# A fused channel-attention and GELU feed-forward kernel: three engines held to one written order, and the fourth feed-forward group of every chunk through the plain second layer

## Chip, core and metric

The kernel runs on one core of a Trainium2 chip. The metric is the device time of one execution in microseconds (us). The kernel before takes 2385.68 us in the median of three runs (2384.44 to 2390.18).

## What is computed

The shapes are four batches of 6080 tokens with 256 channels, all in 32-bit floats, and a feed-forward width of 2048.

```python
qn = q / (norm(q, axis=1) + 1e-6)           # norms over the 6080 tokens
kn = k / (norm(k, axis=1) + 1e-6)
s = kn.transpose(0, 2, 1) @ qn / tau        # 256 x 256 for each batch
a = softmax(s, axis=-1)
x = (v @ a).reshape(4 * 6080, 256)
h = x @ w_in                                # 256 -> 2048
g = 0.5 * h * (1 + erf(h / sqrt(2)))        # GELU
out = g @ w_out                             # 2048 -> 256
```

## The kernel before

**Products in parts.** Each 32-bit operand of a product is split into a high part that TensorE takes as it is and a low part for the rest (`his` and `los` for the activations, `whs` and `wls` for the first layer's weights). A product is then three matmuls: high weights by low activations, high by high, low by high. ScalarE (ACT) makes a high part by a copy or by the GELU itself, and VectorE (DVE) makes the low part by a subtraction, so every low part waits for a copy of ACT.

**Attention.** v @ a @ w_in is done as v @ (a @ w_in), so each batch has its own first-layer weights. While the chunks of batch b run, the kernel also prepares batch b+1: `load_qk`, `split_qk` and `burst` build the 256 x 256 scores, `norm_part` sums the squares for the norms, `softmax` runs in stages, and `w_group` makes the new weights. All this is hung between the steps of batch b by `extras`, by step numbers.

**Steps.** The tokens of a batch are cut in 12 chunks of four times 256 columns (the last two of four times 240), and the 2048 hidden features in 4 groups of 512. A step is one chunk and one group. There are 184 of them, since the first two chunks of the first batch go another way, at the start. In each step the first layer (`chunk_products`) is a Strassen-Winograd scheme: 7 products in place of 8, each 6 matmuls of 256 columns, 42 in all. They accumulate in few PSUM banks: `one` (a buffer of `ph`), `two` (the other buffer of `ph`), `px` and `pz`. Between the products ACT copies `one` to `px` (L585) and `two` to `p` (L590), and DVE adds `one` and `p` into `pz` (L594) and into `p` (L600). The third product (T2) goes on accumulating in `one`, so it may not start before the copy to `px` has read it; the fifth likewise waits for the sum into `pz`, the last for the sum into `p`.

**GELU and the second layer's forms.** Four blocks come out: B22 from `px`, B11 from `p`, B21 from `pz`, B12 from `one`. `block` applies the GELU twice to each, once to full precision into `gs` and once into the high part `his` (L565, L569), and DVE makes `los` (L570). The second layer is again a Strassen-Winograd scheme of 7 products (`chunk_out`), 42 matmuls of 256 columns. It needs four sums of the blocks, T1 to T4, which `sums` makes: three subtractions on DVE (L574, L576, L577), two casts on ACT (L575, L578), two subtractions on DVE (L579, L580). The second layer of a step runs between the first-layer products of the next step (`second`). It gathers four groups in the PSUM banks `po`, and after the fourth the result is joined (L725 to L737) and sent out.

**The plain way.** `plain_out(b, c)` is true for the last chunk of batches 0 to 2. There the second layer is 8 plain products of 3 matmuls with 480 columns, 24 in all, and T1 to T4 are not made. Instead B12 needs its high and low part too.

**What sets the order.** The kernel's calls go to a scheduler, which places each engine's instructions by priority and by a model of the durations, within the data's dependencies. Each engine runs its own list in that order and waits at the first instruction whose operands aren't ready.

**Loads.** Every step reads the second layer's weights again from DRAM (`load_part`, four buffers `wo`, four loads a step, two in a plain one). `norm_part` loads a slice of k or q into the one buffer `kqc` and sums it on ACT (L222) in the same step. All transfers are issued from SyncE (SP).

Of the kernel before, what the change touches and what calls it, by code (L numbers as in the profile page):

```python
# [9 lines left out]
F32 = mybir.dt.float32  # L10
# [38 lines left out]
CROSS = (("S4", "B22"), ("A11", "B11"), ("A12", "B21"), ("S3", "T3"), ("S1", "T1"), ("S2", "T2"), ("A22", "T4"))  # L49
SLOT = {"T2": 0, "T4": 1, "T1": 2, "T3": 3, "B12": 3, "B11": 4, "B22": 5, "B21": 6}  # L50
GSLOT = {"B11": 0, "B12": 1, "B22": 2, "B21": 3}
BLOCK = {(1, 0): "B22", (0, 1): "B11", (1, 1): "B21", (0, 0): "B12"}

# [16 lines left out]
def channel_attention_gelu_ffn(ctx, tc, qk, kqt, vt, tau, w_in, w_out, out):  # L70
# [20 lines left out]
    ps_h = ctx.enter_context(tc.tile_pool(name="ps_h", bufs=2, space=bass.MemoryType.PSUM))  # L91
    ps_x = ctx.enter_context(tc.tile_pool(name="ps_x", bufs=1, space=bass.MemoryType.PSUM))
    ps_o = ctx.enter_context(tc.tile_pool(name="ps_o", bufs=4, space=bass.MemoryType.PSUM))
# [27 lines left out]
    def bank():  # L121
        state["bank"] = at = (state.get("bank", -1) + 1) % 4
        if at % 2 and "halves" not in state:
            return ps_x.tile([P, NT], F32, name="px" if at == 1 else "pz")
        return ps_h.tile([P, NT], F32, name="ph")
# [42 lines left out]
    def qk_fill():  # L168
        state["fill"] = s = ps_o.tile([P, NCT, C], F32, name="po")
# [21 lines left out]
    def split_qk(b, js):  # L191
        raw = raws.pop((b, js))
        hl = pqk.tile([P, 2, JS, 2, C], F32R, name="hl")
        nc.scalar.copy(out=hl[:, 0], in_=raw)
        nc.vector.tensor_tensor(out=hl[:, 1], in0=raw, in1=f32(hl[:, 0]), op=ALU.subtract)
        hls[b, js] = hl


    def burst(b, k, m):
        cs = slice(m * P, (m + 1) * P)  # L200
        s = bank()
        ops = [(hls[b, k * NB + t], j) for t in range(NB) for j in range(JS)]
        for i, (hl, j) in enumerate(ops):
# [3 lines left out]
                             stop=(i == len(ops) - 1), skip_group_check=True)  # L207
        if k == 0:
# [7 lines left out]
    def norm_part(b, t, c):  # L216
# [4 lines left out]
        nc.sync.dma_start(out=x, in_=kqt[b, t, :, c * NS:(c + 1) * NS])  # L221
        nc.scalar.activation(out=x, in_=x, func=AF.Square, accum_out=state["nsum"][:, t, c:c + 1])  # L222

# [10 lines left out]
    def narrow(hi, lo, raw):  # L234
# [7 lines left out]
        else:  # L242
            state["nt"] = not state.get("nt")
            tmp = pg.tile([P, 2, n], F32, name="kqc" if state["nt"] else "pq", bufs=1)
# [37 lines left out]
    def plain_out(b, c):  # L282
        return c == NCH - 1 and b < B - 1

    def parts(b, c):
        return ((1, 3), (6, 8)) if plain_out(b, c) else ((0, 2), (2, 4), (4, 6), (7, 8))

    def load_part(b, c, g, i):
        at, to = parts(b, c)[i]
# [35 lines left out]
    def softmax(first, pool, name):  # L325
# [14 lines left out]
        if first:  # L340
            nps, acc = ps_o.tile([P, NT], F32, name="po"), state.pop("acc")
# [11 lines left out]
        if first:  # L353
            preload(AF.Exp, y)
        nc.vector.reciprocal(out=z, in_=y)
# [9 lines left out]
        rq = pool.tile([P, NT], F32, name=name)  # L365
        nc.tensor.matmul(rq[:, 0:C], ones, diag.rearrange("p h d -> p (h d)"), start=True, stop=True)
        for m in range(NCT):
# [6 lines left out]
        for m in range(NCT):  # L374
            e = pm.tile([P, C], F32, name=f"e{m}")
            den = dens[:, m:m + 1]
            nc.scalar.activation(out=e, in_=ts[m], func=AF.Exp, bias=nms[:, m:m + 1], accum_out=den)
            nc.vector.tensor_scalar(out=den, in0=den, scalar1=1e-9, scalar2=None, op0=ALU.add)
            nc.vector.reciprocal(out=rden[:, m:m + 1], in_=den)
            es.append(e)  # L380
        yield
        tp = pool.tile([P, NT], F32, name=name)
        tpv = tp.rearrange("p (d c) -> p d c", d=NCT)
        for m in range(NCT):
            for d in range(NCT):
                nc.tensor.transpose(out=tpv[:, d, m * P:(m + 1) * P], in_=es[m][:, d * P:(d + 1) * P],
                                    identity=ident)
        eh = pm.tile([P, NCT, C], F32R, name="eh")
        el = pm.tile([P, NCT, C], F32R, name="el")
        marks["eh"] = nc.scalar.copy(out=eh, in_=tpv)  # L390
        if first:
            preload(AF.Gelu, eh[:, 0, 0:2])
        marks["el"] = nc.vector.tensor_tensor(out=el, in0=tpv, in1=f32(eh), op=ALU.subtract)
# [17 lines left out]

    def w_group(b, g):

        eh, el = state["e"]
        win = wins.pop((b, g))
# [3 lines left out]
        for m in range(NCT):  # L419
            cs = slice(m * P, (m + 1) * P)  # L420
            pwt = bank()
            for d in range(NCT):
# [15 lines left out]
    def w_sums(g, tmp, first):  # L438
# [8 lines left out]
        for to, of in ((slice(0, 3), slice(1, 4)), (slice(3, 7), slice(4, 8))):  # L447
            if first and to.start == 0:
                continue
# [515 lines left out]
```

## Time and profile before

| | |
|---|---|
| median of 3 runs | 2385.68 us |
| time of the profiled execution | 2383.55 us |
| its span, first to last instruction | 2381.6 us |
| TensorE: matmuls | 16624 |
| VectorE busy, instructions | 1984.6 us, 2879 |
| ScalarE busy, instructions | 1640.7 us, 2788 |
| bytes moved | 504.51 MB |

PE is TensorE's matmuls and PEld its weight loads, which overlap them. The span lies inside the execution; 1.95 us of the profiled time are outside it. A matmul's row shows a duration longer than the distance to the next matmul, since matmuls overlap in the pipeline. So the work of PE is read from the distance of the starts. A row's text in brackets gives the idle time ahead of it and what ended it.

### The profile page before, as it was taken

What the parts mean: (1) busy time and instruction counts of PE and PEld (TensorE: products, weight loads), DVE (VectorE), ACT (ScalarE), POOL (GpSimd) and SP (SyncE); (2) the same over time, 40 slices, a digit from 0 to 9 for tenths busy, and PEclk for the clock granted to TensorE, in tenths of its full rate; (3) what the DMA queues carried; (4) which work ended last, traced back from release to release, by engine and by line L of the source; (5) the groups of instructions that cost most, each with busy time, mean ns of one, the idle gap of its engine ahead of it and who ended that gap; (6) DMA issues with size and microseconds to landing.
All of it is one profiled execution on the core that took longest, in us unless ns stands there. A gap on an engine that the chain in (4) does not pass through costs nothing.

```text
span 2381.6 us, 42310 instructions
## 1 busy us (share of the span) xinstructions
PE 2225.0 (93%) x16624; PEld 2110.3 (89%) x16624; DVE 1984.6 (83%) x2879; ACT 1640.7 (69%) x2788; POOL 48.5 (2%) x32
## 2 busy tenths in 40 slices
PE   8888999998899999999889999999988999999987
PEld 7768989998889889899879989898988999999987
DVE  6978888898679888889768988788876889899876
ACT  5647777776577677776657777677665667677764
POOL 0250000000000000000000000000000000000000
PEclk9999999999999999999999999999999999999998
DMA  9456777765456676775546677676554565666553
GB/s 379 160 194 234 258 243 261 240 208 177 166 194 226 238 235 233 250 255 191 168 159 206 228 235 245 228 256 230 169 174 144 166 211 191 214 206 207 192 171 133
DMA packets 162406, 504.51 MB, mean 212 GB/s; under 512 B 16672, under 2 KB 26912, under 8 KB 160160
## 3 DMA queue, kind: packets, MB, share of 16 engines
q1 hardware_dynamic: 162208, 501.81, 62.4%
q8 instruction: 131, 2.15, 0.4%
q14 instruction: 67, 0.55, 0.1%
HBM read 464.26 MB, written 37.49 MB: 211 GB/s over the span
## 4 chain that ended last, share of the span: by engine, by line
PE 50%; ACT 15%; DMA 15%; DVE 14%; issue 4%; POOL 1%; SPq 1%; POOLq 0%; ACTq 0%; DVEq 0%
DMA kqc<-kqt 12%; PE po L716 8%; PE po L713 7%; PE po L715 7%; PE ph L555 6%; PE ph L559 5%; PE ph L557 5%; ACT gs L565 4%; ACT his L569 4%; ACT kqc L222 2%; ACT his L578 2%; DVE gs L574 2%; DMA v_raw<-vt 2%; DVE los L580 2%; PE px L555 1%
## 5 line engine op out<-in xcount | busy, mean ns | idle before, releaser
L713 PE MATMUL po<-his,wo 128*128 128x256 f32 (+1 forms) x2408 | 691.6, 289 | 21.2 <-ACT his L578 13.3
L716 PE MATMUL po<-los,wo 128*128 128x256 f32 (+1 forms) x2408 | 677.9, 290 | 21.6 <-DVE los L580 12.2
L715 PE MATMUL po<-his,wo 128*128 128x256 f32 (+1 forms) x2408 | 681.0, 284 | 0.0
L555 PE MATMUL ph<-vhi,wl 128*128 128x256 f32 (+1 forms) x1840 | 533.4, 291 | 79.2 <-ACT px L585 41.9
L570 DVE TENSOR_TENSOR los<-gs,his 128x512 fp32r<-128x512 f32 (+1 forms) x564 | 381.1, 684 | 215.4 <-ACT his L569 211.8
L557 PE MATMUL ph<-vhi,wh 128*128 128x256 f32 (+1 forms) x1840 | 515.1, 280 | 0.0
L559 PE MATMUL ph<-vlo,wh 128*128 128x256 f32 (+1 forms) x1840 | 513.9, 280 | 0.0
L713 PEld LDWEIGHTS po<-his,wo 128*128 128x128 f32 x2408 | 463.1, 192 | 35.0 <-ACT his L578 21.0
L716 PEld LDWEIGHTS po<-los,wo 128*128 128x128 f32 x2408 | 453.4, 192 | 37.4 <-DVE los L580 17.2
L715 PEld LDWEIGHTS po<-his,wo 128*128 128x128 f32 x2408 | 462.4, 192 | 0.2
L555 PEld LDWEIGHTS ph<-vhi,wl 128*128 128x128 f32 x1840 | 350.5, 191 | 104.6 <-ACT px L585 47.2
L557 PEld LDWEIGHTS ph<-vhi,wh 128*128 128x128 f32 x1840 | 351.8, 191 | 1.9
L559 PEld LDWEIGHTS ph<-vlo,wh 128*128 128x128 f32 x1840 | 349.3, 190 | 0.0
L580 DVE TENSOR_TENSOR los<-gs,his 128x1024 fp32r<-128x1024 f32 (+1 forms) x172 | 208.9, 1215 | 54.9 <-ACT his L578 54.4
L578 ACT CAST his<-gs 128x1024 fp32r<-128x1024 f32 (+1 forms) x172 | 178.8, 1040 | 90.0 <-DVE gs L577 88.6
L565 ACT ACTIVATE gs<-px 128x512 f32<-128x512 f32 (+1 forms) x184 | 108.9, 592 | 181.2 <-DVE los L580 83.6
L575 ACT CAST his<-gs 128x1024 fp32r<-128x1024 f32 (+1 forms) x172 | 180.3, 1048 | 52.3 <-DVE gs L574 52.2
L579 DVE TENSOR_TENSOR los<-gs,his 128x1024 fp32r<-128x1024 f32 (+1 forms) x172 | 208.6, 1213 | 7.3 <-ACT his L575 7.0
L574 DVE TENSOR_TENSOR gs<-gs 128x1024 f32<-128x1024 f32 (+1 forms) x172 | 208.4, 1211 | 4.4 <-ACT gs L565 4.2
L590 ACT COPY p<-ph 128x512 f32<-128x512 f32 (+1 forms) x184 | 107.4, 583 | 65.0 <-PE ph L559 64.2
L565 ACT ACTIVATE gs<-p 128x512 f32<-128x512 f32 (+1 forms) x184 | 115.6, 628 | 40.7 <-DVE p L600 40.6
L594 DVE TENSOR_TENSOR pz<-ph,p 128x512 f32<-128x512 f32 (+1 forms) x184 | 126.9, 690 | 18.2 <-PE ph L559 15.2
(248 smaller groups left out, 4195.7 us busy)
## 6 DMA issues: line engine op xcount, KB each, us to landing
wo<-keep_out SPq DMA_DIRECT2D x540, 512.0 KB, 4.2
raw<-qk SPq DMA_DIRECT2D x95, 512.0 KB, 5.7
wo<-keep_out SPq DMA_DIRECT2D x172, 256.0 KB, 4.1
kqc<-kqt SPq DMA_DIRECT2D x72, 512.0 KB, 5.4
v_raw<-vt SPq DMA_DIRECT2D x20, 1024.0 KB, 5.2
out<-osb SPq DMA_DIRECT2D x40, 512.0 KB, 3.0
win<-keep_in SPq DMA_DIRECT2D x12, 1024.0 KB, 4.9
keep_in<-win SPq DMA_DIRECT2D x4, 1024.0 KB, 4.8
```

The lines of the kernel that those rows point to most:

```text
L555: nc.tensor.matmul(o, wls[g][:, a, q], vh[:, at, :h], start=start and q == 0, stop=False, skip_group_check=True)
L557: nc.tensor.matmul(o, whs[g][:, a, q], vh[:, at, :h], start=False, stop=False, skip_group_check=True)
L559: marks["product"] = nc.tensor.matmul(o, whs[g][:, a, q], vl[:, at, :h], start=False, stop=stop, skip_group_check=True)
L565: nc.scalar.activation(out=whole, in_=src, func=AF.Gelu)
L570: tt(out=lo, in0=whole, in1=f32(hi), op=ALU.subtract)
L574: tt(out=t[:, 0:2], in0=t[:, 1:3], in1=t[:, 0:2], op=ALU.subtract)
L578: nc.scalar.copy(out=hi[:, 0:2], in_=t[:, 2:4])
L579: tt(out=lo[:, 2:4], in0=t[:, 0:2], in1=f32(hi[:, 2:4]), op=ALU.subtract)
L580: tt(out=lo[:, 0:2], in0=t[:, 2:4], in1=f32(hi[:, 0:2]), op=ALU.subtract)
L713: nc.tensor.matmul(o, w[:, 1, q], mh, start=first and i % 2 == 0 and q == 0, stop=False, skip_group_check=True)
L715: nc.tensor.matmul(o, w[:, 0, q], mh, start=False, stop=False, skip_group_check=True)
L716: nc.tensor.matmul(o, w[:, 0, q], ml, start=False, stop=last and q == 1, skip_group_check=True)
```

## The change

**One written order.** The chunk loop no longer runs code in the order of its calls. `chunk_ops`, `chunk_out` and `join_ops` return small functions, each for one operation or one product. For every step they get a planned time, PE's products one after another at `D` = 0.71 apart, the operations of ACT and DVE at offsets from the ends of the products. The work for the next batch and the next chunk (`later`) gets places in the same plan. The list is sorted by planned time and emitted in that order, and each instruction of PE, ACT and DVE (`PINNED`) is bound to follow the one before it on its engine. SP's and POOL's instructions stay with the scheduler. The start of the program, up to the first step, is not bound.

**Group 4 is plain.** `plain_out(g)` is now true for group index 3 of each chunk of each batch, and no longer depends on the chunk. 46 steps are plain, against 12 before; 3 are plain in both. For 43 steps T1 to T4 go away, and 9 steps that were plain (groups 0 to 2 of the last chunk in batches 0 to 2) get them. The products of a chunk are gathered in other halves of the banks (`PLACE`), so that the plain products add into banks `po0` and `po1`, and the join needs two copies and five sums.

**Buffers and places.** The PSUM banks get fixed names: `pa` and `pb` take the place of the two buffers of `ph` and change roles at every step. `p5` has one buffer in place of two, and `pq` is gone into a larger `osb`. The load of `kqc` is planned one step ahead of its sum (`norm_load`, `norm_sum`), and `raw` is split one block in each step rather than two in one. The loads of `wo` are taken from one list (`todo`), always four ahead.

```diff
+PINNED = (mybir.EngineType.PE, mybir.EngineType.Activation, mybir.EngineType.DVE)
...
-    def plain_out(b, c):
-        return c == NCH - 1 and b < B - 1
+    def plain_out(g):
+        return g == NWG - 1
...
-    def chunk_products(b, c, g):
+    def chunk_ops(c, g, n):
...
+            if i == 0:
+                new("one", ps_h, "pb" if n % 2 else "pa")
+            if i == 1:
+                state["spare"] = "pa" if n % 2 else "pb"
+                new("two", ps_h, state["spare"])
...
+        copy, join = join_ops(b, c)
+        put(n + 1, "act0", copy, 2)
+        put(n + 1, "act0", copy, 3)
+        put(n + 1, "dve0", join, 0)
+        put(n + 1, "dve0", join, 1)
+        put(n + 1, "o5", join, 2)
+        put(n + 1, "dve3", join, 3)
+        put(n + 2, "dve1", join, 4)
...
+        for i in range(2 * NCT * NSC):
+            put(n0 + 8 + i, "load", norm_load, b, *divmod(i, NSC))
+            put(n0 + 9 + i, "act2", norm_sum, b, *divmod(i, NSC))
...
+    D = 0.71
...
+        if len(outs) == 8:
+            row = [0, "o", "o", 1, "o", 2, "x", "o", 3, "o", 4, "x", "o", 5, "o", 6, "o"]
+        else:
+            row = [0, "o", 1, "o", 2, "x", "o", 3, "o", 4, "x", "o", 5, "o", 6, "o"]
...
+        at(e[0] + .05, x_copy)
+        at(e[1] + .05, p5_copy)
+        at(e[2] + .1, z_add)
...
+        at(e[3] + .05, gelu_hi, "B22")
+        at(e[3] + .5, gelu_whole, "B22")
+        spread(n, "act2", e[3] + 1.05)
+        at(e[3] + 1.1, lo, "B22")
+        at(e[4] + .1, p5_add)
...
+        at(e[4] + .8, gelu_hi, "B11")
+        at(e[4] + 1.3, gelu_whole, "B11")
+        at(e[4] + 1.85, lo, "B11")
...
+        at(e[5] + .4, gelu_hi, "B21")
+        at(e[5] + .9, gelu_whole, "B21")
+        at(e[5] + 1.5, lo, "B21")
+        at(e[6] + .1, gelu_whole, "B12")
+        if plain_out(g):
+            at(e[6] + .6, gelu_hi, "B12")
+            at(e[6] + 1.2, lo, "B12")
+        else:
+            at(e[6] + .7, t_add, 0)
+            at(e[6] + 1.85, t_hi, 0)
+            at(e[6] + 1.85, t_add, 1)
+            at(e[6] + 2.45, t_add, 2)
+            at(e[6] + 3.05, t_lo, 0)
+            at(e[6] + 3.1, t_hi, 1)
+            at(e[6] + 5.0, t_lo, 1)
...
+    for _, _, fn, args in sorted(plan, key=lambda x: x[:2]):
+        fn(*args)
+        for ins in body[seen:]:
+            if ins.engine in PINNED:
+                if ins.engine in latest:
+                    tc.add_manual_dep(ins, latest[ins.engine], mybir.DependencyInfo(
+                        mybir.DependencyClass.NoSync, mybir.DependencyReason.DATA), reason="order")
+                latest[ins.engine] = ins.name
+        seen = len(body)
```

In the plan, `e[i]` is the planned end of first-layer product i, "o" a product of the step before's second layer, and "x" a place for one piece of the next batch's TensorE work (half a burst, for one).

ACT's list at a border of two steps in the last chunk, before. `gs<-ph` is the GELU of B12, which ends a step; the two casts make the high parts of T1 to T4; the copies `px<-ph` and `p_25489<-ph` (the tile `p`) belong to the next step's first layer.

```order
L565 ACTIVATE gs<-ph 128x2x240
L575 CAST his<-gs 128x4x240
L578 CAST his<-gs 128x4x240
L585 COPY px<-ph 128x2x240
L590 COPY p_25489<-ph 128x2x240
```

The same place of ACT's list in the changed kernel (`pa` and `pb` are the two banks that were `ph`; L672 is the cast, L631 and L635 the copies).

```order
L652 ACTIVATE gs<-pb 128x2x240
L631 COPY px<-pa 128x2x240
L672 CAST his<-gs 128x4x240
L635 COPY p_24498<-pb 128x2x240
L672 CAST his<-gs 128x4x240
```

The copy to `px` has moved ahead of both casts, and the copy to `p` between them.

DVE's list at the same border, before: the three subtractions of the sums, the low parts of T1 to T4 (L579, L580), the next step's sum into `pz` (L594), and then its low parts and the sum into `p` (L600).

```order
L574 TENSOR_TENSOR gs<-gs 128x4x240
L576 TENSOR_TENSOR gs<-gs 128x2x240
L577 TENSOR_TENSOR gs<-gs 128x2x240
L579 TENSOR_TENSOR los<-gs,his 128x4x240
L580 TENSOR_TENSOR los<-gs,his 128x4x240
L594 TENSOR_TENSOR pz<-ph,p_25489 128x2x240
L570 TENSOR_TENSOR los<-gs,his 128x2x240
L600 TENSOR_TENSOR p_25489<-ph,p_25489 128x2x240
```

DVE's list there in the changed kernel (L665 to L669 are the subtractions, L676 the low parts of T1 to T4, L639 the sum into `pz`, L642 that into `p`).

```order
L665 TENSOR_TENSOR gs<-gs 128x4x240
L667 TENSOR_TENSOR gs<-gs 128x2x240
L669 TENSOR_TENSOR gs<-gs 128x2x240
L676 TENSOR_TENSOR los<-gs,his 128x4x240
L639 TENSOR_TENSOR pz<-pa,p_24498 128x2x240
L676 TENSOR_TENSOR los<-gs,his 128x4x240
L658 TENSOR_TENSOR los<-gs,his 128x2x240
L642 TENSOR_TENSOR p_24498<-pa,p_24498 128x2x240
```

The sum into `pz` has moved between the two low parts; the rest keeps its order.

More of the change, by code (lines that the diff above doesn't have):

```diff
@@ L594, in chunk_products @@
-        tt(out=z, in0=one, in1=p5, op=ALU.add)
-        yield
-        do(3, x, False, True)
-        block((1, 0), x)
-        yield
-        do(4, one, False, False)
-        tt(out=p5, in0=one, in1=p5, op=ALU.add)
-        block((0, 1), p5)
-        yield
-        do(5, z, False, True)
-        block((1, 1), z)
-        yield
-        do(6, one, False, True)
-        yield
-        block((0, 0), one)
-        if not plain:
-            sums()
+                start, stop = i < 2 and q == 0, i not in (0, 2, 4)
@@ new lines, in z_add, with p5_add, whole, slot @@
+        def z_add():
+            new("z", ps_x, "pz")
+            tt(out=t["z"], in0=t["one"], in1=t["p5"], op=ALU.add)
+        def p5_add():
+            tt(out=t["p5"], in0=t["one"], in1=t["p5"], op=ALU.add)
+        def whole(name):
+            return halves(gs[:, GSLOT[name]], h)
+        def slot(name):
+            at = (PSLOT if plain else SLOT)[name]
+            return [halves(x[:, at], h) for x in (his, los)]
+        def gelu_whole(name):
+            nc.scalar.activation(out=whole(name), in_=t[SOURCE[name]], func=AF.Gelu)
@@ L612, in channel_attention_gelu_ffn, with t_hi, t_lo @@
+        def t_hi(i):
+            nc.scalar.copy(out=views[1][:, 2 - 2 * i:4 - 2 * i], in_=views[0][:, 2 * i:2 * i + 2])
+        def t_lo(i):
+            at = slice(2 - 2 * i, 4 - 2 * i)
+            tt(out=views[2][:, at], in0=views[0][:, 2 * i:2 * i + 2], in1=f32(views[1][:, at]), op=ALU.subtract)
+        return do, x_copy, p5_copy, z_add, p5_add, gelu_whole, gelu_hi, lo, t_add, t_hi, t_lo
+    SOURCE = {"B22": "x", "B11": "p5", "B21": "z", "B12": "one"}
     po = {}
@@ L688, in chunk_out @@
[L688 to L689 removed]
+                    mh, ml = (halves(m[:, SLOT[v]], h)[:, q] for m in (his, los))
+                    nc.tensor.matmul(o, w[:, 1, q], mh, start=starts and q == 0, stop=False, skip_group_check=True)
                     nc.tensor.matmul(o, w[:, 0, q], mh, start=False, stop=False, skip_group_check=True)
[L691 removed]
@@ new lines, in channel_attention_gelu_ffn, with spread @@
+    for n, (b, c, g) in enumerate(steps):
+        if g != NWG - 1:
+            continue
+        copy, join = join_ops(b, c)
[7 more added lines that the diff above has]
+    D = 0.71
+    now, previous, tail = 0.0, list(second), 0.0
+    T_BASE = 10000.0
+    def spread(n, kind, t, d=0.01):
+        for i, (fn, args) in enumerate(later.pop((n, kind), [])):
+            at(t + i * d, fn, *args)
```

562 lines of the change are left out of this document (312 added, 250 removed).

## The prediction

> **What bounds the kernel now.** I read the page first, then busy time by stretches (one per batch), then the waits of PE, then single places in time. The page's rows: span, busy time by engine, and the granted clock in 40 slices.
>
> ```profile
> span 2381.6 us, 42310 instructions
> PE 2225.0 (93%) x16624; PEld 2110.3 (89%) x16624; DVE 1984.6 (83%) x2879; ACT 1640.7 (69%) x2788; POOL 48.5 (2%) x32
> PEclk9999999999999999999999999999999999999998
> ```
>
> PE is the busiest, but its 93% contains overlap, so I count its work from the starts of matmuls. A stretch without waits gives the distance for 256 columns; pairs of rows give the others. In the windows the columns are us, then busy time (and instructions) of PE, PEld, DVE, ACT and POOL, the clock, the DMA share and GB/s.
>
> ```profile
> 2010.00:2020.00 10.00, 10.00 (x85) 9.92 (x84) 9.15 (x14) 8.16 (x15) 0.00 (x0) 1.00 0.63 197
> ```
> ```profile
> 173.90 0.40 PE L516 MATMUL px<-vlo,wh 128*128 128x512 f32 x1
> 174.13 0.40 PE L633 MATMUL po<-his,wo 128*128 128x512 f32 x1
> ...
> 999.69 0.39 PE L204 MATMUL ph<-hl 128*128 128x512 f32 x1
> 999.92 0.28 PE L206 MATMUL ph<-hl 128*128 128x256 f32 x1
> 1000.04 0.39 PE L204 MATMUL ph<-hl 128*128 128x512 f32 x1
> ...
> 1847.70 0.38 PE L689 MATMUL po<-his,wo 128*128 128x480 f32 x1
> 1848.79 0.38 PE L691 MATMUL po<-los,wo 128*128 128x480 f32 x1
> ...
> 2302.00 0.28 PE L555 MATMUL ph<-vhi,wl 128*128 128x240 f32 x1
> 2302.67 0.27 PE L713 MATMUL po<-his,wo 128*128 128x240 f32 x1
> ```
>
> So a matmul of 256 columns takes 0.118 (10 us / 85), of 512 columns 0.233, of 480 columns 0.218 (1.09 / 5), of 240 columns 0.111 (0.67 / 6), and a burst's pair 0.35. By batch:
>
> ```profile
> 175.00:675.00 500.00, 463.05 (x3504) 439.15 (x3504) 414.81 (x600) 355.36 (x605) 3.42 (x4) 0.98 0.65 221
> 675.00:1266.00 591.00, 551.10 (x4211) 526.15 (x4210) 492.42 (x707) 415.62 (x705) 0.00 (x0) 0.99 0.64 216
> 1266.00:1856.00 590.00, 551.54 (x4204) 526.89 (x4203) 492.05 (x706) 414.58 (x703) 0.00 (x0) 0.98 0.63 211
> 1856.00:2376.00 520.00, 503.01 (x4057) 493.36 (x4056) 440.56 (x624) 353.57 (x608) 0.00 (x0) 0.98 0.57 189
> ```
>
> PE's work in a middle batch: 10 chunks x 4 steps x 84 x 0.118 = 396.5; the two narrow chunks 504 x 0.111 = 55.9 and 96 plain matmuls x 0.218 = 20.9; 12 bursts of 8 pairs, 33.6; 48 matmuls for the next weights, 11.2. That is 518.1 of 591 and of 590. The first batch has 8 wide chunks, 10 bursts and 24 matmuls left over from the start: 317.2 + 55.9 + 20.9 + 28.0 + 11.2 + 5.6 = 438.8 of 500. The last batch has only steps: 396.5 + 672 x 0.111 = 471.1 of 520. PE therefore works **1946 us and loses 255** (61 + 73 + 72 + 49) between 175 and 2376 us. DVE, at most 85% busy by batch, isn't full. What the loss is made of, the waits of PE show in part:
>
> ```profile
> PE ph L555 <- ACT px L585: 41.9, 21, 4.1
> PE po L713 <- ACT his L578: 13.3, 15, 1.7
> PE po L716 <- DVE los L580: 12.2, 20, 0.8
> ...
> PE ph L555 <- DVE el L393: 7.6, 3, 2.6
> ...
> PE ph L555 <- ACT gs L524: 3.5, 1, 3.5
> ```
>
> The columns are the total, the number and the longest. The largest is the third product waiting for the copy to px, and a place near the end shows why:
>
> ```profile
> 2292.40 1.15 DVE L574 TENSOR_TENSOR gs<-gs 128x960 f32<-128x960 f32 x1
> ...
> 2293.59 1.00 ACT L575 CAST his<-gs 128x960 fp32r<-128x960 f32 x1 [1.33 <-DVE gs L574]
> ...
> 2294.01 0.27 PE L559 MATMUL ph<-vlo,wh 128*128 128x240 f32 x1
> ...
> 2295.03 0.99 ACT L578 CAST his<-gs 128x960 fp32r<-128x960 f32 x1 [0.44 <-PE po L716]
> 2295.93 0.55 ACT L585 COPY px<-ph 128x480 f32<-128x480 f32 x1
> ...
> 2296.53 0.38 PE L555 MATMUL ph<-vhi,wl 128*128 128x240 f32 x1 [1.58 <-ACT px L585]
> ```
>
> The copy stands behind two casts that wait for DVE. ACT sat idle 1.33 us and then PE 1.58, at a place where neither was short of time. The loss is one of order and of the chain through T1 to T4.
>
> **The change: PE's work.** A step made plain swaps 42 matmuls of 256 for 24 of 512: 24 x 0.233 - 42 x 0.118 = +0.64. There are 38 of these. Of the narrow steps 5 become plain and 9 cease to be: -4 x (24 x 0.218 - 42 x 0.111) = -4 x 0.57. Together +24.2 - 2.3 = **+22 us**, so 1968.
>
> **DVE and ACT.**
>
> ```profile
> L580 DVE TENSOR_TENSOR los<-gs,his 128x1024 fp32r<-128x1024 f32 (+1 forms) x172 | 208.9, 1215 | 54.9 <-ACT his L578 54.4
> L579 DVE TENSOR_TENSOR los<-gs,his 128x1024 fp32r<-128x1024 f32 (+1 forms) x172 | 208.6, 1213 | 7.3 <-ACT his L575 7.0
> L574 DVE TENSOR_TENSOR gs<-gs 128x1024 f32<-128x1024 f32 (+1 forms) x172 | 208.4, 1211 | 4.4 <-ACT gs L565 4.2
> L577 DVE TENSOR_TENSOR gs<-gs 128x512 f32<-128x512 f32 (+1 forms) x172 | 117.5, 683 | 1.4
> L570 DVE TENSOR_TENSOR los<-gs,his 128x512 fp32r<-128x512 f32 (+1 forms) x564 | 381.1, 684 | 215.4 <-ACT his L569 211.8
> L600 DVE TENSOR_TENSOR p<-ph,p 128x512 f32<-128x512 f32 (+1 forms) x184 | 125.4, 681 | 8.3 <-PE ph L559 6.0
> L565 ACT ACTIVATE gs<-px 128x512 f32<-128x512 f32 (+1 forms) x184 | 108.9, 592 | 181.2 <-DVE los L580 83.6 <-PE px L559 75.3 <-PE ph L559 18.5
> ```
>
> A plain step saves DVE 1.211 + 2 x 0.683 + 1.213 + 1.215 = 5.0 and adds one low part of 0.684: -4.3, over 34 steps net about -146 us. ACT loses two casts and gains one GELU. I count neither as gained time, since neither engine is the bound; both buy slack. The join stays as large as it was (five sums for six) and hides under the plain step's missing sums.
>
> **The order.** Can ACT and DVE keep up with PE at 84 x 0.118 = 9.9 us a step? The longest ring goes through both: three subtractions, first low part, sum into pz, second low part (1.211 + 0.683 + 0.683 + 1.213 + 0.68 + 1.215 = 5.7); the full-precision GELU of B22, which writes where the second low part reads (0.59); low part of B22 and sum into p (0.684 + 0.681 = 1.37); two GELUs each of B11 and B21 and one of B12 (5 x 0.59 = 2.95). That is 10.6, against 9.9; rows of one engine that don't wait for each other overlap somewhat (ACT's row at 2295.93 starts 0.09 before its predecessor's end), about 8 such places, so 9.9 to 10.6. Each of three borders in a chunk may thus run late by 0 to 0.7; the fourth, behind the plain step, has no T sums and catches up. The plan leaves slack: the sum into p is planned 0.1 after product five, and the last product comes three places of 0.71 later, 2.1 less 0.1 and less the sum's 0.68, so 1.3. Late by at most 3 x 0.7 = 2.1, plus 0.7 for the v and join pieces in the second step, less 1.3: **0 to 1.5 us a chunk**. At the chunk's first step ACT has two v splits and two join copies (about 0.5 each, as the copy of 0.55 above) ahead of the copy to px, which may add up to 1.5 where the lateness isn't recovered. So 0 to 3 a chunk; I take **1.3, that is 60 us for 46 chunks** (it was 255 / 46 = 5.5), the value nearest to the ring's upper end.
>
> **Other terms.** The start isn't bound: 175 us stay. The wait in the first step (3.5 for L524) stays, since the weight preparation ahead of it is the same, and I allow as much again less 1 for what follows from it there: 6. The softmax between batches is now spread over five steps, so PE's waits for el (7.6 over three batches) shrink, but its pieces are extra work in ACT's and DVE's lists: 4 a batch, 12 us (bounds 6 to 20). SP gets no new transfers; plain steps load two parts in place of four. The end:
>
> ```profile
> 2376.03 0.41 PE L716 MATMUL po<-los,wo 128*128 128x240 f32 x1
> ```
>
> From there to the span's end are 5.6 us of join and store; the join is as long, so they stay. **Sum:** 175 + 1968 + 60 + 6 + 12 + 5.6 = 2226.6. The profiled execution has 1.95 outside its span, and its 2383.55 lies 2.1 below the median of 2385.68, which I ignore. **2228 us.**
>
> **The clock.**
>
> ```profile
> 2000.00:2100.00 100.00, 100.00 (x814) 98.20 (x814) 88.73 (x125) 71.46 (x123) 0.00 (x0) 1.00 0.61 200
> ...
> 2320.00:2340.00 20.00, 15.80 (x109) 15.61 (x110) 12.36 (x19) 9.46 (x19) 0.00 (x0) 0.83 0.43 143
> ```
>
> Where PE runs without gaps the clock is 1.00; where it waits long it falls to 0.83. My distances are those at 1.00, and the 255 lost contain the slower stretches. If the first three batches kept 0.98 by short waits, the 1490 us of work there would take 30 more, 2258. [...]
>
> **Rivals.** (1) The order leaves almost no waits: 0.3 a chunk, 6 and 6: 175 + 1968 + 14 + 12 + 5.6 + 2 = 2177. For it speaks the window 2000 to 2100, where 814 matmuls ran almost without a gap; against it the ring. Chance 0.17. (2) DVE becomes the bound. With the saving its busy time is some 391 + 460 + 460 + 391 = 1702 us by batch (1840 less 146, plus some 8 for the join). If in a fixed list it keeps only 80% busy in the first three batches, these take 1311 / 0.80 = 1639 and the last 485: with the ends 182.6, 2307. The window 2000 to 2100 shows 88.7% in the old order, so it can do better. Chance 0.13. (3) **Slower: ACT held by the loads of kqc.**
>
> ```profile
> ACT kqc L222 <- DMA kqc<-kqt: 81.7, 60, 3.5
> ```
> ```profile
> kqc<-kqt SPq DMA_DIRECT2D x72, 512.0 KB, 5.4
> ```
>
> ACT waited 60 times of 72. The sum is now bound between the GELU of B22 and that of B11; there is one buffer, so each load waits for the sum before. If a load comes late, all that stands behind it on ACT waits, and PE for that a step later. The plan gives a load about one step, 9.9 less some 1.2 for the sum itself (the cast of like width took 1.00), against 5.4 from issue to landing, so 3 us to spare. Only if SP's list holds the loads back by those 3 and 2.2 more each does the gain of 155 us go (72 x 2.2). At 3.5 each, the longest wait now, all 72 passed on: 2228 + 252 = 2480. The far end, the longest wait passed on each time, is not likely with 3 us to spare. Chance 0.04.
>
> **How the numbers follow.** The forecast, with waits of 0.7 to 2.2 a chunk (2200 to 2270), has 0.65; the rivals 0.17, 0.13 and 0.04; 0.01 for no change. The range takes in rival 1 below (2177). The bounds of the unknown costs reach 2315 above (138 + 6 + 20 of waits), which needs all of them at their end at once; I stop at **2300**, and at **2172** below. Left out are then most of rival 2 and all of rival 3. Faster by over 0.3% (what a measurement of this kernel can tell from none) 0.95, within 0.01, slower 0.04.
>
> **What would show it.** Right: the four batches take about 466, 543, 543 and 494 us in place of 500, 591, 590 and 520; no wait of the third product for the copy to px above a few us in total; DVE below 90%; the clock at 0.99 or more in all batches. Wrong: ACT's waits for kqc as large as before with PE's waits a step behind them; PE waiting for the sum into p or pz in each step, as the ring would have it; a plain second layer whose 24 matmuls take more than 5.6 us.

## The result and the profile after

The changed kernel takes **2235.96 us** in the median of four runs (2234.12 to 2237.01), the kernel before 2385.06 in four runs beside it (2383.4 to 2390.18). The ratio is **0.9371**, with a 95% interval of 0.9354 to 0.9387: 149 us less, where 2228 us (157 less) had been forecast. The profiled execution took 2234.12 us.

The page of the kernel after, its span, busy time by engine and granted clock in 40 slices:

```profile
span 2232.3 us, 40801 instructions
PE 2179.1 (98%) x16012; PEld 2050.7 (92%) x16012; DVE 1886.7 (85%) x2712; ACT 1599.6 (72%) x2714; POOL 46.3 (2%) x32
PEclk9999999999999999999999999999999999999999
```

The span is 149 us shorter while PE's busy time fell by 46 only: most of what went is PE's waiting (busy 93% of the span before, 98% now). The same stretches as before, one per batch (columns as in the prediction's windows):

```profile
182.90:633.60 450.70, 441.38 (x3360) 422.50 (x3359) 383.16 (x545) 338.80 (x575) 0.00 (x0) 0.99 0.66 225
633.60:1178.10 544.50, 535.10 (x4064) 509.95 (x4063) 468.65 (x668) 405.90 (x687) 0.00 (x0) 1.00 0.66 222
1178.10:1722.50 544.40, 535.09 (x4065) 509.98 (x4064) 468.67 (x668) 405.88 (x688) 0.00 (x0) 1.00 0.65 218
1722.50:2227.60 505.10, 503.54 (x3853) 477.80 (x3852) 412.77 (x585) 343.29 (x594) 0.00 (x0) 1.00 0.54 179
```

The first batch begins 8 us later than before; 5.6 of them are the 24 matmuls left over from the start, which now run ahead of its first step and not inside it. The middle batches take 46 us less, the last 15. The longest waits of PE now (total, number, longest):

```profile
PE pb L625 <- DVE p L642: 5.8, 14, 1.1
PE pa L170 <- DMA raw<-qk: 5.7, 3, 3.6
PE po L703 <- ACT his L581: 5.1, 2, 3.3
```

The wait of the third product for the copy to px, 41.9 us before, is gone from the list; ACT's wait for the loads of `kqc`, 81.7 before, is gone too. What is left inside the steps is the ring through ACT and DVE. One border of two steps in the last batch shows it, DVE's rows first (start, duration), ACT's behind them:

```profile
1831.95 1.22 DVE L665 TENSOR_TENSOR gs<-gs 128x1024 f32<-128x1024 f32 x1
...
1836.28 1.22 DVE L676 TENSOR_TENSOR los<-gs,his 128x1024 fp32r<-128x1024 f32 x1
1838.16 0.69 DVE L658 TENSOR_TENSOR los<-gs,his 128x512 fp32r<-128x512 f32 x1 [0.66 <-ACT gs L652]
1838.77 0.68 DVE L642 TENSOR_TENSOR p<-pa,p 128x512 f32<-128x512 f32 x1
1840.67 0.69 DVE L658 TENSOR_TENSOR los<-gs,his 128x512 fp32r<-128x512 f32 x1 [1.22 <-ACT gs L652]
...
1842.25 1.22 DVE L665 TENSOR_TENSOR gs<-gs 128x1024 f32<-128x1024 f32 x1
```
```profile
1837.53 0.60 ACT L652 ACTIVATE gs<-px 128x512 f32<-128x512 f32 x1 [0.94 <-DVE los L676]
1839.48 0.63 ACT L655 ACTIVATE his<-p 128x512 fp32r<-128x512 f32 x1 [1.36 <-DVE p L642]
...
1841.50 0.60 ACT L652 ACTIVATE gs<-pa 128x512 f32<-128x512 f32 x1
```

Read it as a relay. DVE's second low part (1836.28) releases ACT's full-precision GELU of B22 (1837.53), that releases DVE's low part (1838.16), behind which stands the sum into p (1838.77), that releases ACT's GELUs of B11 (1839.48), and behind those and the GELUs of B21 ends that of B12 (1841.50), which the next L665 needs (1842.25). One turn takes 1842.25 - 1831.95 = 10.30 us against the 9.9 of PE's matmuls. Either engine waits 0.7 to 1.4 us at each handover and both look far from full. The list of PE's waits barely shows the loss, as a matmul's row is 0.28 long at a distance of 0.118, so that small delays disappear in the overlap; the length of the step shows it.

### The profile page after: what moved, and what is told of

Same layout as the page of the kernel before. It is cut to its first block, busy times and chain, and to the rows that moved or that the text cites. A ratio compares the mean times of both kernels' runs of the same rounds, so it can differ in the third digit from the quotient of the medians.

```text
span 2232.3 us, 40801 instructions
## 1 busy us (share of the span) xinstructions
PE 2179.1 (98%) x16012; PEld 2050.7 (92%) x16012; DVE 1886.7 (85%) x2712; ACT 1599.6 (72%) x2714; POOL 46.3 (2%) x32
## 4 chain that ended last, share of the span: by engine, by line
PE 66%; DVE 17%; ACT 9%; issue 5%; DMA 2%; POOL 1%; SPq 0%; ACTq 0%; POOLq 0%; DVEq 0%
PE po L756 7%; PE po L758 7%; PE po L757 7%; PE pa L625 4%; PE pb L625 4%; PE pb L627 3%; PE pb L626 3%; PE pa L626 3%; PE pa L627 3%; PE po L742 3%; DVE gs L665 3%; PE po L740 3%; PE po L741 3%; DVE los L676 2%; ACT gs L652 2%
## 5 line engine op out<-in xcount | busy, mean ns | idle before, releaser
L756 PE MATMUL po<-his,wo 128*128 128x256 f32 (+1 forms) x1932 | 544.9, 282 | 0.0
L757 PE MATMUL po<-his,wo 128*128 128x256 f32 (+1 forms) x1932 | 542.9, 281 | 0.0
L756 PEld LDWEIGHTS po<-his,wo 128*128 128x128 f32 x1932 | 367.0, 190 | 3.1
L757 PEld LDWEIGHTS po<-his,wo 128*128 128x128 f32 x1932 | 364.2, 189 | 0.8
L672 ACT CAST his<-gs 128x1024 fp32r<-128x1024 f32 (+1 forms) x276 | 288.1, 1044 | 80.5 <-DVE gs L665 80.5
L676 DVE TENSOR_TENSOR los<-gs,his 128x1024 fp32r<-128x1024 f32 (+1 forms) x276 | 332.6, 1205 | 0.0
L625 PE MATMUL pa<-vhi,wl 128*128 128x256 f32 (+1 forms) x920 | 263.2, 286 | 9.2 <-DVE small L414 3.4
L625 PE MATMUL pb<-vhi,wl 128*128 128x256 f32 (+1 forms) x920 | 263.5, 286 | 8.3 <-DVE p L642 5.8
L626 PE MATMUL pa<-vhi,wh 128*128 128x256 f32 (+1 forms) x920 | 256.9, 279 | 0.0
L627 PE MATMUL pa<-vlo,wh 128*128 128x256 f32 (+1 forms) x920 | 256.7, 279 | 0.0
L626 PE MATMUL pb<-vhi,wh 128*128 128x256 f32 (+1 forms) x920 | 256.2, 278 | 0.0
L627 PE MATMUL pb<-vlo,wh 128*128 128x256 f32 (+1 forms) x920 | 256.2, 278 | 0.0
L625 PEld LDWEIGHTS pa<-vhi,wl 128*128 128x128 f32 x920 | 174.5, 190 | 25.3 <-DVE p L642 6.5
L626 PEld LDWEIGHTS pa<-vhi,wh 128*128 128x128 f32 x920 | 174.7, 190 | 4.4
```

Of the source, the lines that this page charges most:

```text
L625: nc.tensor.matmul(o, wls[g][:, a, q], vh[:, at, :h], start=start, stop=False, skip_group_check=True)
L626: nc.tensor.matmul(o, whs[g][:, a, q], vh[:, at, :h], start=False, stop=False, skip_group_check=True)
L627: nc.tensor.matmul(o, whs[g][:, a, q], vl[:, at, :h], start=False, stop=stop, skip_group_check=True)
L672: nc.scalar.copy(out=views[1][:, 2 - 2 * i:4 - 2 * i], in_=views[0][:, 2 * i:2 * i + 2])
L676: tt(out=views[2][:, at], in0=views[0][:, 2 * i:2 * i + 2], in1=f32(views[1][:, at]), op=ALU.subtract)
L756: nc.tensor.matmul(o, w[:, 1, q], mh, start=starts and q == 0, stop=False, skip_group_check=True)
```

## The experiments

Eleven kernels were run, each beside runs of the kernel before. "Step" is the distance from one step's first matmul to the next's, "us a chunk" a batch's time by its chunks. None leaves out a part of the computation. Experiments 2 to 11 keep the change's fixed banks and its spread of `raw`, so what these two are worth isn't separated.

### 1. The plain group alone

The kernel before with the change's `plain_out(g)` (and the places and the join that it needs), in the scheduler's order.

```diff
-    def plain_out(b, c):
-        return c == NCH - 1 and b < B - 1
+    def plain_out(g):
+        return g == NWG - 1
```

> The kernel before, with its scheduler's order, and only the fourth group of each chunk through the plain second layer (and the join that this needs). If the order makes the gain (the theory of the prediction), TensorE has the same 22 us more of work as in the changed kernel, and the waits fall only where the T sums go, at one border in four: 2340 to 2390 us. If the lighter load of VectorE and ScalarE makes it, most of the gain appears here: 2240 to 2290 us.

Measured: 2359.09 us, ratio 0.9912 (0.9883 to 0.994). This is what was expected if the order makes the gain. The longest wait of its PE, then of its ACT:

```profile
PE ph L557 <- ACT px L587: 21.9, 17, 2.1
```
```profile
ACT kqc L224 <- DMA kqc<-kqt: 78.4, 51, 3.0
```

DVE has the changed kernel's sums (1886.4 us busy) and PE the changed kernel's matmuls, yet the waits stay. The lighter load alone is worth 1%, in the scheduler's order.

### 2. The order alone

The changed kernel with no plain group. The join, which the plain step had made room for, goes behind the last product.

```diff
     def plain_out(g):
-        return g == NWG - 1
+        return False
...
-        put(n + 1, "act0", copy, 2)
-        put(n + 1, "act0", copy, 3)
-        put(n + 1, "dve0", join, 0)
-        put(n + 1, "dve0", join, 1)
+        put(n + 1, "act2", copy, 2)
+        put(n + 1, "o5", copy, 3)
+        put(n + 1, "o5", join, 0)
+        put(n + 1, "o5", join, 1)
         put(n + 1, "o5", join, 2)
-        put(n + 1, "dve3", join, 3)
+        put(n + 1, "o5", join, 3)
```

> The changed kernel with its bound order, but no plain group: all four groups through the seven products, and the join moved a step later, behind the last of these. If the order makes the gain, TensorE's work is 22 us less than in the changed kernel and the ring through ScalarE and VectorE, which now never catches up, costs some 0.2 to 0.5 us more at each of 184 borders: 2240 to 2300 us. If the lighter load makes it: over 2320 us, with VectorE over 90% busy in the middle batches.

Measured: **2394.07 us, ratio 1.0051 (1.0028 to 1.0075).** The expectation failed by 94 us at its nearer end: this order alone gains nothing. The time is that of the other theory, but its sign is missing: DVE is busy 514 of 583 us, 88%, in the second batch, and over 90% had been asked. In the last batch the steps take 12.5, 12.7, 10.3 and 10.3 us, again and again, so the loss sits in the first two steps of each chunk. DVE's rows at these two borders:

```profile
1976.81 1.22 DVE L665 TENSOR_TENSOR gs<-gs 128x1024 f32<-128x1024 f32 x1
1977.95 0.69 DVE L545 TENSOR_TENSOR vs<-v_raw 128x512 f32<-128x512 f32 x1
...
1979.47 0.68 DVE L667 TENSOR_TENSOR gs<-gs 128x512 f32<-128x512 f32 x1
...
1988.67 0.43 DVE L784 TENSOR_TENSOR osb<-osb 128x256 f32<-128x256 f32 x1 [0.27 <-ACT osb L778]
...
1990.93 0.68 DVE L658 TENSOR_TENSOR los<-gs,his 128x512 fp32r<-128x512 f32 x1
1991.53 1.22 DVE L665 TENSOR_TENSOR gs<-gs 128x1024 f32<-128x1024 f32 x1
```

The sums of the next chunk's v (1.5 us) stand between the first and the second subtraction of the T sums, and four sums of the join (2.3 us from 1988.67) ahead of a low part and of L665: both inside the ring, which they lengthen. In the changed kernel they stand at the border behind the plain step, which has no T sums, so there they are outside the ring. So two theories stood against each other: the plain group is worth its gain by the **places** that it makes, or by DVE's lighter **load**.

### 3. The same plan, not bound

The changed kernel, sorted by the same plan, but no instruction is bound to follow the one before.

```diff
-            if ins.engine in PINNED:
+            if False:
```

> The changed kernel, emitted in the same planned order, but without binding the instructions to it, so that the scheduler may place them by its own priorities again. If the binding matters, casts come ahead of the copy to px again and the time is 2290 us or more. If the plan and its places of the calls are enough, it stays within 10 us of 2236.

Measured: 2428.17 us, ratio 1.0202 (1.0175 to 1.0228). PE waits again for the copy to px (22.8 and 22.2 us in its two largest groups). The first batch of this run, columns as before:

```profile
184.30:758.00 573.70, 477.13 (x3359) 447.85 (x3358) 385.21 (x557) 389.74 (x671) 0.00 (x0) 0.90 0.66 219
```

Its profiled execution is 184 us longer than that of the changed kernel. 123 of them are lost in this batch, and only there does ACT wait for the loads of `kqc` (101.6 us in all). A middle batch takes 27 us more, nearly all of it in its last two chunks (in the third batch 116.2 us for the two, 90.5 in the changed kernel). In chunks 3 to 9 of that batch the unbound list is as fast as the bound one, 314.9 us for 313.1. So the binding is needed at some places, and not at every step.

### 4. The copies to px and p behind the casts of the T sums

```diff
-        at(e[0] + .05, x_copy)
-        at(e[1] + .05, p5_copy)
+        at(max(e[0] + .05, start + 2.45), x_copy)
+        at(max(e[1] + .05, start + 2.46), p5_copy)
```

> The changed kernel with the copies to px and to p planned behind both casts of the T sums, the order that ScalarE had in the kernel before; nothing else is moved by hand. If that place is what TensorE waited for, the copy ends some 1.2 to 1.5 us too late at each of 138 borders with T sums: 2236 + 160 to 200, so 2390 to 2440 us, with the third product waiting for the copy. If the ring sets the pace anyway and the place of the copy hardly matters, under 2270 us.

Measured: 2563.27 us, ratio 1.0774 (1.0722 to 1.0827), 327 us above the changed kernel; 2390 to 2440 were expected, so the direction was right and the size too small. The edit moves two copies, to px and to p. The waits of its PE:

```profile
PE pb L625 <- ACT px L631: 174.7, 92, 3.3
PE pa L625 <- ACT px L631: 82.9, 46, 3.3
```

PE waits at every border with T sums, 92 + 46 = 138 times and 1.87 us each, 258 of the 327. That the rest is a longer ring, by the later GELUs, is only argued. Behind both casts at every border, the two copies cost more than the whole gain. It doesn't follow that the kernel before had them there at every border; it hadn't, as is shown further down.

### 5 and 6. One row moved out of the ring

The low part of B22 stands ahead of the sum into p on DVE, though ACT waits for the sum. Experiment 5 moves it behind the sum in the changed kernel, experiment 6 in the kernel of experiment 2.

```diff
-        at(e[3] + 1.1, lo, "B22")
         at(e[4] + .1, p5_add)
+        at(e[4] + .15, lo, "B22")
```

> The changed kernel with one move in VectorE's list: the low part of B22 comes right behind the sum into p instead of ahead of it. No work is added or taken away. If the ring through ScalarE and VectorE (10.3 us at a border with T sums) sets the remaining waits, it loses the GELU of B22 and that low part, some 1.2 us, falls below TensorE's 9.9, and most of the about 1.4 us a chunk that TensorE still loses goes: 2170 to 2205 us. If the waits come from the engines' load, nothing changes: 2225 to 2245 us.

> The same move in the kernel of the second experiment (bound order, no plain group). If its slowness is the ring, which is never broken there and has the join's and v's pieces in it, each of four borders a chunk gets up to 1.2 us shorter: 2394 falls by 100 to 180 us, to 2215 to 2295. If VectorE's load is the bound, it stays over 2350 us.

Measured: 2202.38 us, ratio **0.9227 (0.9213 to 0.9241)**, for experiment 5, the fastest of all kernels here, and 2325.11 us, 0.9743 (0.9728 to 0.9758), for experiment 6. With the plain group the last batch's steps go from 11.0, 10.1, 10.3 and 10.3 to 10.5, 10.0, 10.0 and 10.0, which is PE's work: the ring was the bound of these steps. Without it the bare borders fall to 10.0 as well, but the step with the join keeps 12.3, and the gain was 69 us where 100 to 180 were expected; the time lies between the ranges of both theories. Middle and last batch of experiment 6, then of experiment 5:

```profile
652.20:1221.50 569.30, 540.67 (x4280) 524.25 (x4279) 509.94 (x716) 422.36 (x699) 0.00 (x0) 0.99 0.70 229
1793.10:2315.20 522.10, 498.48 (x4088) 486.82 (x4086) 459.44 (x632) 364.26 (x607) 0.00 (x0) 1.00 0.61 193
```
```profile
628.00:1166.00 538.00, 531.68 (x4064) 509.90 (x4063) 464.85 (x668) 406.49 (x687) 0.00 (x0) 1.00 0.68 225
...
1703.50:2195.70 492.20, 490.89 (x3854) 476.70 (x3853) 413.29 (x585) 345.05 (x594) 0.00 (x0) 1.00 0.58 184
```

### 7 and 8. DVE's load put back, inside the ring or beside it

Both recompute low parts in the changed kernel, 160 us more of DVE's busy time in experiment 7, 155 in experiment 8. Experiment 7 makes the first T low part twice (138 times, 1.14 us each), in the ring; experiment 8 the low part of B22 two more times (138 times, 1.22 together), behind the sum into p.

```diff
+            at(e[6] + 3.06, t_lo, 0)
```
```diff
+        if not plain_out(g):
+            at(e[4] + .15, lo, "B22")
+            at(e[4] + .16, lo, "B22")
```

> The changed kernel with the first low part of the T sums computed twice in a row (the same values), in steps with T sums: VectorE works 138 x 1.14 = 157 us more, all of it in the ring, ahead of the sum into pz. If the ring sets the pace: 60 to 140 us more than 2236 (the plain step and the steps with a burst take some of it up). If load counts, it costs no more than the next kernel does.

> The changed kernel with the low part of B22 computed two more times (the same values) behind the sum into p, in the same steps: VectorE works 138 x 1.22 = 168 us more, at the place where it otherwise waits 1.2 us for ScalarE's GELU of B11. If the ring sets the pace: at most 25 us more than 2236. If load counts: as much as the kernel before this one, or more.

Measured: 2364.68 us (0.9906, 0.9888 to 0.9924) and 2310.71 us (0.968, 0.9665 to 0.9695). That is 129 more than the changed kernel in the ring and 75 more beside it; 60 to 140 and at most 25 were expected, so the second missed. A middle and the last batch of experiment 7, then of 8:

```profile
658.20:1233.70 575.50, 551.20 (x4064) 513.75 (x4063) 511.54 (x704) 406.40 (x688) 0.00 (x0) 1.00 0.64 210
1808.80:2359.30 550.50, 517.80 (x3854) 480.81 (x3852) 456.76 (x621) 343.30 (x594) 0.00 (x0) 1.00 0.52 165
```
```profile
653.40:1222.30 568.90, 542.89 (x4065) 511.39 (x4064) 510.09 (x740) 405.95 (x688) 0.00 (x0) 1.00 0.65 213
1791.10:2305.30 514.20, 506.77 (x3854) 478.39 (x3852) 455.40 (x657) 343.12 (x594) 0.00 (x0) 1.00 0.56 176
```

In the last batch place is nearly all: 43 to 44 us more of DVE's busy time cost 45 us inside the ring and 9 beside it. In the middle batches, where DVE also has the splits and sums for the next batch, 41 us more cost 24 even beside the ring (43 more cost 31 inside it). The cost falls on some steps only. The steps of chunks 3 to 5 of the second batch, in us (those over 13 have a burst):

| | chunk 3 | chunk 4 | chunk 5 |
|---|---|---|---|
| changed kernel | 10.49, 13.11, 10.03, 10.03 | 13.30, 10.00, 10.03, 13.28 | 10.49, 10.48, 13.41, 10.03 |
| experiment 8 | 10.49, 14.47, 10.03, 10.31 | 13.82, 10.00, 11.06, 14.15 | 10.49, 11.80, 14.19, 10.03 |

It is paid in the steps with a burst and in some steps ahead of one. In the step of 11.80 DVE has no room left, with 11.70 us busy:

```profile
858.54:870.34 11.80, 10.87 (x85) 10.21 (x84) 11.70 (x18) 8.11 (x13) 0.00 (x0) 1.00 0.88 289
```

So load counts where a single step of DVE is full; the share of a whole batch doesn't show it.

### 9 and 11. Better places without a plain group

Experiment 9 is experiment 6 with the join and the pieces of v away from the borders; ACT copies three of the four banks, and DVE still reads the remaining one, `po1`, from PSUM.

```diff
+        put(n + 1, "act2", copy, 0)
+        put(n + 2, "act0", copy, 3)
+        for i in range(4):
+            put(n + 2, "dve2", join, i)
+        put(n + 2, "dve2", join, 4)
...
+        put(n + 2, "dve2", v_sums, nb, nc_)
+        for part in range(2, 4):
+            put(n + 3, "act", v_hi, nb, nc_, part)
+            put(n + 3, "dve2", v_lo, nb, nc_, part)
```

> Bound order without a plain group, with the sum into p first and with the join and the pieces for the next chunk's v taken off the ring: they stand behind the sum into p, where VectorE waits for the GELU, and bank 0 is copied out at once, so that the next chunk's second layer needn't wait for the join. TensorE has 22 us less work than with a plain group. If the places alone make the gain, this comes near 2202 less 22: 2175 to 2210 us. If the plain group is also needed for VectorE's load (45.7 us busy a chunk in the middle batches of the last such run, against 43.2 of TensorE's work), VectorE sets the pace there, at 46 to 48 us a chunk: 2225 to 2290 us.

Measured: 2337.45 us, 0.9781 (0.9754 to 0.9807), above both theories and above experiment 6. One wait of its PE tells why:

```profile
PE po L756 <- DVE osb L792: 69.3, 33, 5.4
```

The next chunk's first product into `po1` has to wait until the last sum of the join (L792) has read it, and this sum now came too late: a wait that my own placing made. Experiment 11 lets ACT copy that bank as well (into a ninth part of `osb`), so that no product waits for a sum of the join.

```diff
+            if k == 1:
+                nc.scalar.copy(out=o[:, 8], in_=banks(1)[:, 1])
...
-                tt(out=o[:, 3], in0=banks(1)[:, 1], in1=o[:, 3], op=ALU.add)
+                tt(out=o[:, 3], in0=o[:, 8], in1=o[:, 3], op=ALU.add)
...
-        put(n + 2, "act0", copy, 3)
+        put(n + 2, "act", copy, 3)
+        put(n + 2, "act", copy, 1)
```

> The one written order without any plain group, as in the run before it (no plain group, join and v sums off the border), but ACT copies the fourth PSUM bank too, and the copies of the last two banks stand ahead of the GELU of B22, so that no matmul waits for the sums of the join. In the run before, PE waited 69.3 us in 33 places (up to 5.4) for the last of these sums, always at the first product of the next chunk's fourth bank. Nothing is left out of the computation. Theory of places (what costs time is only what stands in the ring or holds a bank): that wait goes, and the middle batches fall from 48.3 us a chunk to 44.5 to 45.5; PE's work is 1939 us, 29 less than with the plain group, and with 184 ahead, 7 behind and waits as in the best run so far (some 43) it is 2173; range 2160 to 2225. Theory of DVE's load (510 us of sums in a middle batch of 580, the plain group is needed to lighten it): DVE does not get above about 91% there as in the run with join and v sums still at the border, so 560 a batch and at least 2270. A time between 2225 and 2270 speaks for neither alone.

Measured: **2300.7 us, 0.9628 (0.9604 to 0.9652)**, the best that was found without the plain group. Its second and last batch (the third takes 569.9):

```profile
656.70:1224.40 567.70, 536.70 (x4281) 521.45 (x4279) 510.59 (x716) 428.74 (x723) 0.00 (x0) 0.99 0.70 230
1794.30:2291.40 497.10, 490.66 (x4088) 484.99 (x4086) 457.28 (x635) 374.83 (x632) 0.00 (x0) 1.00 0.64 203
```

The theory of places holds in the last batch: 497 us, 56 below experiment 2 and within 5 of experiment 5. It falls in the middle batches, where DVE's 510 us take 568 to 570. The theory of load had said 560 or more. Experiments 6, 8 and 11, with their extra sums at quite different places, all end there, with DVE busy 90%, but it isn't shown that one bound sets all three. In the second batch, PE's longest wait in experiment 6 comes at a bank that the join reads (17.3 us in 8 places, put down to ACT's copy to px; the last section shows one), in experiments 8 and 11 that of bursts for the bank that ACT's copy to p frees (9.9 in 9, 13.3 in 12).

### 10. The load of kqc in the same step as its sum

```diff
-            put(n0 + 8 + i, "load", norm_load, b, *divmod(i, NSC))
+            put(n0 + 9 + i, "load", norm_load, b, *divmod(i, NSC))
```

> The changed kernel with the load of kqc planned in the same step as its sum again, as in the kernel before. If the step of lead is what removed ScalarE's 82 us of waits for kqc, ScalarE waits 1 to 3 us at each of 72 sums and TensorE loses part of it: 2255 to 2330 us. If the transfer lands in time anyway, within 8 us of 2236.

Measured: 2236.74 us, 0.9361 (0.9333 to 0.9388), like the changed kernel. ACT's wait for these loads in this run:

```profile
ACT kqc L240 <- DMA kqc<-kqt: 1.5, 2, 1.0
```

So the lead of one step isn't what removed the 81.7 us of waits; in the bound order they stay away without it.

## Why the prediction was right, and where it was not

The time was forecast within 0.4%, and its sum holds, by batch too. It rests on PE's work and on the ring of the changed kernel, not on what held the kernel before. Of that the prediction read only a part, and its reading that the plain group's relief is no gained time was wrong.

- **What bounded the kernel before.** Read from one place, and true of such places only. All but 0.3 of the 41.9 us of waits for the copy to px lie in the last two chunks of a batch, those of 240 columns, where that place is. Chunks 3 to 9 and 11 to 12 of the third batch, then chunks 2 to 10 of the last, before and after:

```profile
1352.67:1698.98 346.31, 325.33 (x2515) 310.91 (x2513) 298.67 (x420) 254.99 (x431) 0.00 (x0) 0.99 0.70 233
1740.66:1856.10 115.44, 98.05 (x669) 90.73 (x670) 77.95 (x126) 68.66 (x122) 0.00 (x0) 0.94 0.46 156
1896.57:2268.16 371.59, 371.55 (x3027) 365.04 (x3026) 333.34 (x477) 266.32 (x459) 0.00 (x0) 1.00 0.62 203
```
```profile
1272.92:1586.05 313.13, 311.19 (x2373) 298.78 (x2372) 273.31 (x373) 242.70 (x411) 0.00 (x0) 1.00 0.71 240
1632.03:1722.49 90.46, 88.03 (x679) 82.12 (x677) 74.26 (x117) 66.68 (x119) 0.00 (x0) 1.00 0.57 191
1767.97:2142.98 375.01, 374.88 (x2865) 356.27 (x2863) 308.20 (x433) 256.30 (x442) 0.00 (x0) 1.00 0.55 182
```

  In the wide chunks of the last batch nothing was gained: PE hardly waited there before, and at a border in them the copy to px (2197.07) already stood ahead of the casts (2198.79). The third batch gains 33 us in chunks 3 to 9 and 25 in its last two, and loses 12 in the other three. Chunks 3 to 9 are those with the sums of `kqc`. ACT waited 30 us for these loads there, waits that the prediction named as a rival only and left out of the loss. With them gone but no plain group this stretch takes 335.1 us (experiment 2), with the plain group but the waits kept 338.3 (experiment 1), with both, though unbound, 314.9 (experiment 3). What the waits alone were worth stays open, as no run has them in the bound order.
- **The sum.** PE's work of 1968 us less the 5.6 that moved ahead of the first step is 1962; with 182.9 ahead of that step and 4.7 behind the last matmul, 83 us are left as lost of the span of 2232.3. Forecast were 60 + 6 + 12 = 78. Some 11 of the 83 are PE's own: a step of 256 columns with 42 matmuls in either layer takes 10.0 us where PE never waits (experiment 5), not 9.9, and there are 114 of them. The start came out 2.3 us longer than forecast (7.9 later, 5.6 of it moved work), the end 0.9 shorter.
- **By batch.** Forecast 466, 543, 543 and 494, measured 450.7, 544.5, 544.4 and 505.1. The windows don't hold equal work, though: 12 weight matmuls and 24 of the plain second layer (2.8 + 5.2 us) run behind the end of each batch that has one after it, so the first window lacks 8.0 and the last has 8.0 more (3853 matmuls, of which 3816 are its own). Besides, the 5.6 us left over from the start are not in the first. With this PE's work is 429.2, 523.4, 523.4 and 486.6, and 21.5, 21.1, 21.0 and 18.5 are lost. Forecast were 23, 19.6, 19.6 and 15.6, so the term is right in size and in its place.
- **The ring.** Forecast 9.9 to 10.6 us a border, measured 10.30 on the trace, and experiments 5 and 7 shorten and lengthen the steps with it. A wide chunk of the last batch takes 41.7 us, and 40.6 in experiment 5, where the ring is shorter: it cost 1.1 a chunk, within the forecast 0 to 1.5. That the 1.3 taken came so close is in part luck, as nothing in the prediction singled it out within 0 to 3.
- **"I count neither as gained time, since neither engine is the bound; both buy slack."** This is the step that failed. The sum didn't need it to be right, but as a cause it isn't: with the first bound order and no plain group nothing is gained (2394), with better places 89 us (2300.7), and only with the plain group 149 to 184. In the middle batches 510 to 514 us of DVE's work took 568 us or more in every order that was tried, and the plain group takes that load to 465 to 469 and the batch to 538 to 544. In the last batch it matters by the places that it leaves for the join and v.
- **DVE's saving.** 146 less 8 was forecast by the rows' durations. From the pages it is 1984.6 - 1886.7 = 98. Neighbouring rows overlap (the sum into p at 1838.77 starts 0.08 before the row ahead of it ends), so a row adds less busy time than it lasts; whether that is all of the difference wasn't looked into.
- **The clock.** The prediction counted at 1.00; that short waits would leave it there was its author's estimate. Measured is 0.99 or 1.00 in every batch, as forecast, and the 2258 of a clock at 0.98 did not come. The waits of 1.72 and 3.22 us in the stretch from 2320 to 2340, where it had been 0.83, are gone.
- **Rival 1, almost no waits (2177).** Not in the changed kernel, but experiment 5 (2202) goes more than half of the way by one moved row.
- **Rival 2, DVE as the bound (2307).** Not with the plain group (86% busy in the middle batches); without it DVE is 90% busy in them at best, rather than 80%, and full in single steps; that this sets their time isn't shown.
- **Rival 3, the loads of kqc (2480).** They no longer hold ACT; experiment 10 shows that there was room for even less lead. What their going was worth is open, as said above.

**Open.** In the last batch of experiment 11 DVE was busy 457 of 497 us, 92%, so the 90% of the middle batches are no limit of DVE as such. In the middle batches the next batch's splits and sums fall on some steps and its bursts on others; whether a smoother spread could go below 568 us without the plain group was not tried. Experiment 8 shows that load costs time in a step where DVE is full (11.80 us in place of 10.48, with DVE busy 11.70). That 510 us of it set 568 is not shown, and for experiments 6 and 11 only argued from their like times.

## What to carry to other kernels

Where PE waits and neither ACT nor DVE is full, follow the relay between the two for one turn and compare its length with PE's work in a step; in the last batch of experiments 7 and 8, 43 to 44 us more of DVE's work cost 45 us inside it and 9 beside it, where DVE had room. Test a change of order and a change of load apart: here the load alone gave 1%, the order alone nothing at first and 4% with better places, both together 6 to 8%. Before calling one wait the bound, see in which chunks it occurs and which chunks the change makes shorter. A bank that is read late can cost as much as an instruction placed wrongly (69.3 us of PE's waits in experiment 9); copy it out early if the next group needs it.

## What the runs showed of the hardware

In experiment 9 the matmuls ran slower for a while behind one of the waits for the fourth bank:

```profile
1414.33 0.38 PE L756 MATMUL po<-his,wo 128*128 128x256 f32 x1 [2.24 <-DVE osb L792]
...
1414.79 0.41 PE L756 MATMUL po<-his,wo 128*128 128x256 f32 x1
...
1418.20 0.28 PE L626 MATMUL pb<-vhi,wh 128*128 128x256 f32 x1
```

Behind 2.24 us of idleness the distance of two matmuls was 0.21 in place of 0.118, for the 16 matmuls from 1414.79 to 1418.20. They took 3.41 us, some 1.5 more than 16 x 0.118. In experiment 6 PE waited 2.15 us at a like place, and the two distances behind the second matmul are 0.11 and 0.12:

```profile
1428.47 0.35 PE L756 MATMUL po<-his,wo 128*128 128x256 f32 x1 [2.15 <-ACT px L631]
1428.67 0.28 PE L757 MATMUL po<-his,wo 128*128 128x256 f32 x1
1428.78 0.28 PE L758 MATMUL po<-los,wo 128*128 128x256 f32 x1
1428.90 0.28 PE L756 MATMUL po<-his,wo 128*128 128x256 f32 x1
```

The granted clock (third from the end) in two neighbouring stretches there, in experiment 9 and then in experiment 6:

```profile
1411.36:1414.77 3.41, 1.17 (x10) 0.97 (x9) 3.31 (x7) 1.35 (x3) 0.00 (x0) 1.00 0.86 259
1414.77:1418.19 3.42, 3.42 (x18) 3.42 (x17) 3.23 (x5) 1.19 (x2) 0.00 (x0) 0.50 0.98 367
```
```profile
1423.98:1427.39 3.41, 2.35 (x18) 2.14 (x18) 3.11 (x5) 3.41 (x8) 0.00 (x0) 1.00 0.77 208
1427.39:1430.81 3.42, 2.34 (x20) 2.37 (x21) 3.32 (x6) 0.76 (x3) 0.00 (x0) 1.00 0.92 338
```

In experiment 9 the clock was 1.00 in the stretch that holds the wait and 0.50 in the next. In experiment 6, whose wait lies partly in each, it was 1.00 in both. What decides between the two isn't shown.

The releaser named for the wait in experiment 6, ACT's copy to px, is hardly the one that ended it. DVE's sum of the join, which reads a bank, ran until just before the matmul:

```profile
1427.68 0.69 DVE L788 TENSOR_TENSOR osb<-po,osb 128x512 f32<-128x512 f32 x1
```

It ends at 1428.37, the matmul starts at 1428.47. Where the named engine has long been done (the copy ran from 1427.30 for 0.64), look for another reader of the same bank.
